# Moving one weight load behind two casts, and the first second products behind two sets of transposes

## The chip, the cores and the metric

The kernel runs on one core of one Trainium2 chip. The metric is device microseconds of one launch, taken as the median of several runs; lower is better. A separate execution is recorded by the hardware profiler, and all engine times below come from that one.

## What is computed

A linear attention with a decay per head is followed by a two-layer network without gating. Four sequences of 768 positions, 8 heads of 64, give 3072 tokens of width 512.

```python
for b in range(nb):                      # blocks of 64 positions
    intra = (qb @ kb.T * Dmask) @ vb     # Dmask[i, j] = lam ** (i - j) for i >= j
    inter = (qb * lam_pow) @ kv_state
    out[block] = intra + inter
    kv_state = lam_block * kv_state + (kb * rev_pow).T @ vb
x = out as (3072, 512)
h = x @ w_in                             # 512 x 2048
g = max(h, 0) + alpha * min(h, 0)
y = g @ w_out                            # 2048 x 512
```

Inputs and the output are float32. Inside, matrix products take float16 and accumulate in float32.

## The kernel before

The tokens are cut into 6 chunks of 512 (two sequences, 256 positions each). A chunk holds four *units*: unit `4c + 2*bi + hh` is sequence `bi` of the chunk's two and head half `hh` (4 heads). So units 4 and 5 share one set of loaded q, k and v (`load(1, 0, ...)`), and units 6 and 7 another (`load(1, 1, ...)`).

Each unit goes through these steps:

- `load(c, bi, x)` (L87) brings q, k or v of two units from HBM, on SyncE's DMA queue: 0.5 MB in float32.
- `cast(n, name, engine)` makes float16 of one unit's k, q or v; the engine is `G` (GpSimd, L252), `A` (ScalarE, L248) or `V` (VectorE, L250).
- `key_decayed(n)` (L278) makes the decayed key.
- `transposes(n, engine)` turns q and k round. For `A` and `V` it is eight TensorE transposes into the PSUM bank `tk` (L306) and a copy out by that engine. For `D` it is a transposing DMA on SyncE's queue (L296). `decayed(n)` (L340) makes the decayed query from the result.
- `cluster(old, new)` is TensorE's attention work: the state's part of `old` (L367), the scores of `new` (L384), scores times v of `old` (L396), and the state's update from decayed key and v of `new` (L411). VectorE masks the scores (L422) and VectorE and ScalarE move the state (L443 to L447); then the output of `old` is copied into `xT`.

Once four units of a chunk are through, the network follows: `up(c, f)` (L479) is one of 16 first products of a chunk, 4 matmuls of 128x512, with ScalarE's part (L487) and VectorE's `slope_product` (L503) behind it. `down(c, t, part, 4)` (L518) is a fourth of the second product for token tile `t`: 4 matmuls that read w_out's quarter `part`. The last part is copied out by ScalarE (L531) and stored by SyncE (L540); with `hold` the store is issued later, by `store_held`. The last chunk uses `down_last` (L547).

Weights are loaded in quarters on GpSimd's DMA queue, with a cast from float32 to float16 under way: `load_win(i)` (L96) and `load_wout(i)` (L102), 0.5 MB each as written. `gate(i, "out")` (L113) is a tiny copy on SyncE's queue that reads a quarter: SyncE stands there until the quarter has landed, and the loads behind it start no earlier.

The order on every engine is the program's order, written out by hand for chunks 0 to 2: each engine, and each DMA queue, takes its instructions as they come in the text and waits on semaphores. Buffers are rotating: 5 sets of raw tiles, 4 of each float16 tile, 3 output tiles; PSUM has banks `op`, `tk`, `acc`, two `h`, and two for scores. GpSimd issues w_out's loads between its casts, so a cast that waits for its data also holds back the loads behind it.

Of the kernel before, what the change touches and what calls it, by code (L numbers as in the profile page):

```python
# [11 lines left out]
def kernel(  # L12
# [67 lines left out]
    def load(c, bi, x, half=None):  # L80

        pb, b = c // 2, 2 * (c % 2) + bi
        if (c, bi) not in raws:
            raws[c, bi] = [raw_pool.tile([128, H, 2 * D], fp32, tag=f"{n}raw", name=f"{n}raw") for n in "kqv"]
        heads = ds(0, H) if half is None else ds(4 * half, 4)
        i = "kqv".index(x)
        nc.sync.dma_start(  # L87
            out=raws[c, bi][i][:, heads, :],
            in_=(k, q, v)[i][b, heads, ds(pb * W, W), :].rearrange("h (p e) d -> p h (e d)", e=2),
        )  # L90
# [10 lines left out]
    def load_wout(i):  # L101
        nc.gpsimd.dma_start(  # L102
            out=w_out_sb[:, ts(i, 4), :],
            in_=moe_w_out[ts(i, 512), :].rearrange("(f p) d -> p f d", p=128),
        )
# [20 lines left out]
    def bank_of(bank, name, dtype=fp32):  # L126
        pool = h_ps_pool if bank == "h" else ps
        return pool.tile([128, CH], dtype, tag=bank, name=name)
# [101 lines left out]
    def query_decay(hp, block):  # L230
        x = qdecay[:, hp // 2, :, hp % 2, ds(block * 64, 64)]
        f = pos_f.rearrange("p (e a j) -> p e a j", e=2, a=2)[:, :, block]
        nc.scalar.activation(x, f, AF.Exp, scale=llp[:, hp : hp + 1])
# [12 lines left out]
    def copy_on(eng, out, in_):  # L246
        if eng == "A":
            nc.scalar.activation(out, in_, AF.Copy)  # L248
        elif eng == "V":
            nc.vector.tensor_copy(out=out, in_=in_)  # L250
        else:
            nc.gpsimd.tensor_copy(out=out, in_=in_)  # L252

    def raw_of(n):
        c, bi, hh = units[n]
        return {
            x + "16": t[:, ds(4 * hh, 4), :].rearrange("p h (e d) -> p e h d", e=2)
            for x, t in zip("kqv", raws[c, bi])
        }

    def cast(n, name, eng):
        t = T.setdefault(n, {})
        if name == "v16":
            t[name] = half_pool.tile([128, 2, 4, D], fp16, tag=name, name=name)
            copy_on(eng, t[name], raw_of(n)[name])
            return
        if "qk16" not in t:
            t["qk16"] = half_pool.tile([128, 2, 2, 4, D], fp16, tag="qk16", name="qk16")
        copy_on(eng, t["qk16"][:, int(name == "k16")], raw_of(n)[name])

    def engine(x):
        return nc.gpsimd if x == "G" else nc.vector

    def key_decayed(n, eng="G"):
        hh = units[n][2]
        kr = raw_of(n)["k16"]
        kdec = half_pool.tile([128, 2, 4, D], fp16, tag="kdec", name="kdec")
        engine(eng).tensor_tensor(  # L278
            out=kdec,
            in0=kr,  # L280
            in1=kdecay[:, ds(4 * hh, 4), :].rearrange("p h e -> p e h").unsqueeze(3).to_broadcast([128, 2, 4, D]),
            op=ALU.mult,
        )
        T.setdefault(n, {})["kdec"] = kdec
# [6 lines left out]
    def transposes(n, eng, decay=True):  # L291

        t = T[n]
        qkT = qkt_pool.tile([128, 2, 2, 2, L], fp16, tag="qkT", name="qkT")
        if eng == "D":
            nc.sync.dma_start(  # L296
                out=qkT.rearrange("p x e h j -> p (x e h) j"),
                in_=t["qk16"].rearrange("p x e h d -> p (x e h d)"),
                transpose=True,
            )  # L300
        else:
            tp = ps.tile([128, 2, 2, 2, L], fp16, tag="tk", name="tp")
            for x in (1, 0):
                for e in range(2):
                    for hp in range(2):
                        nc.tensor.transpose(  # L306
                            tp[:, x, e, hp, :],
                            t["qk16"][:, x, e, ds(2 * hp, 2)].rearrange("p l d -> p (l d)"),
                            ident,
                        )  # L310
            copy_on(eng, qkT, tp)
            t["qps"] = tp[:, 0]
        t["qkT"] = qkT
        if decay:
            decayed(n)
# [19 lines left out]
    def decayed(n, eng="G"):  # L335
        c, bi, hh = units[n]
        t = T[n]
        qdT = qkt_pool.tile([128, 2, 2, L], fp16, tag="qdT", name="qdT")
        p = ds(64, 64) if c < 2 else ds(0, L)
        engine(eng).tensor_tensor(  # L340
            out=qdT[:, :, :, p],
            in0=(t["qps"] if eng == "P" else t["qkT"][:, 0])[:, :, :, p],
            in1=qdecay[:, hh, :, :, p],
            op=ALU.mult,
        )
        t["qdT"] = qdT
# [123 lines left out]
    G = {}  # L470
# [21 lines left out]
    def slope_product(c, f, bi=None):  # L492
        h_ps, m = OPEN.pop((c, f, bi))
        n = CH if bi is None else W
        if (c, f) not in G:
            G[c, f] = g_pool.tile([128, 2, 2, L], fp16, tag=f"g{f}", name=f"g{f}")
        g = G[c, f]
        if bi is None:
            g, mv, hv = g.rearrange("p e b j -> p (e b j)"), m, h_ps
        else:  # L500
            g = g[:, :, bi, :]
            mv, hv = (y[:, 0:n].rearrange("p (e j) -> p e j", e=2) for y in (m, h_ps))
        nc.vector.scalar_tensor_tensor(  # L503
            out=g, in0=mv, scalar=oma[:, f : f + 1], in1=hv, op0=ALU.mult, op1=ALU.add
        )

    def lhs(c, f, t):
        return G[c, f][:, t // 2, t % 2, :]
# [3 lines left out]
    def down(c, t, part, nparts, bank="op", hold=False):  # L512
        if part == 0:
            O[c, t] = bank_of(bank, "o_ps")
        o_ps = O[c, t]
        n = NF // nparts
        for f in range(part * n, part * n + n):
            nc.tensor.matmul(  # L518
                o_ps,
                lhsT=lhs(c, f, t),  # L520
                rhs=w_out_sb[:, f, :],
                start=(f == 0),
                stop=(f == NF - 1),
            )
        if part == nparts - 1:
            store(c, t, o_ps, 0, DM, hold)
            del O[c, t]

    def store(c, t, o_ps, c0, n, hold=False):
        o_sb = o_pool.tile([128, DM], fp32, tag="osb", name="o_sb")  # L530
        nc.scalar.activation(o_sb[:, 0:n], o_ps[:, 0:n], AF.Copy)  # L531
        pb, b = c // 2, 2 * (c % 2) + t % 2
        rows = out[ds(b * S + pb * W, W), ds(c0, n)].rearrange("(j e) d -> e j d", e=2)[t // 2]
        HELD[c, t] = (rows, o_sb[:, 0:n])
        if not hold:
            store_held(c, t)

    def store_held(c, t):
        rows, tile = HELD.pop((c, t))
        nc.sync.dma_start(out=rows, in_=tile)  # L540
# [141 lines left out]
    slope_product(0, 7, None)  # L682
    up(0, 4, None, "h", True)
    slope_product(0, 4, None)
    load_wout(0)
    up(0, 11, None, "op")
    key_decayed(4, "G")
    up(0, 8, None, "tk")
# [3 lines left out]
    up(0, 14, None, "h")  # L692
    cast(4, "v16", "G")
    load(1, 1, "q", None)
    cast(7, "k16", "G")
    cast(5, "k16", "V")
    up(0, 5, None, "op", True)
# [12 lines left out]
    up(0, 12, None, "h", True)  # L710
    cast(6, "k16", "A")
    load_wout(3)
    down(0, 0, 0, 4, "h")
    cast(5, "v16", "G")
    slope_product(0, 12, None)
    gate(3, "in")
    cluster(4, 5, "V", state_first=True)
    cast(6, "q16", "G")
    transposes(6, "A", False)
    key_decayed(6, "G")  # L720
    down(0, 2, 0, 4, "op")
    load(2, 0, "k", None)
    down(0, 3, 0, 4, "h")
    cast(7, "q16", "G")
    transposes(7, "V", False)
    decayed(7, "V")
    decayed(5, "V")
    down(0, 2, 1, 4, "op")
# [4 lines left out]
    cluster(5, 6, "A", state_first=True)  # L733
    decayed(6, "V")
    cast(7, "v16", "A")
    load(2, 1, "q", None)
    cast(11, "q16", "G")
    down(0, 1, 0, 4, "tk")
    down(0, 2, 2, 4, "op")
    down(0, 0, 1, 4, "h")  # L740
    load(2, 0, "q", None)
    cast(9, "k16", "G")
    cast(8, "q16", "G")
    cluster(6, 7, "A")
    load(2, 1, "k", None)
    key_decayed(10, "G")
# [10 lines left out]
    key_decayed(9, "G")  # L757
    up(1, 6, None, "op")
    transposes(8, "D", False)
    load(3, 0, "k", None)  # L760
    down(0, 0, 3, 4, "h", True)
    down(0, 3, 2, 4, "h")
    store_held(0, 0)
    query_decay(1, 0)
    cast(10, "k16", "A")
    decayed(8, "G")
    cast(9, "q16", "A")
    up(1, 5, None, "tk", True)
    transposes(9, "D", False)
    cast(11, "k16", "G")  # L770
    slope_product(1, 5, None)
    up(1, 7, None, "op", True)
# [11 lines left out]
    up(1, 4, None, "op")  # L784
    up(1, 11, None, "h")
    load(2, 1, "v", None)
    cluster(8, 9, "A")
    transposes(10, "D", False)
    up(1, 9, None, "tk")
# [158 lines left out]
```

## Time and profile before

| | us |
|---|---|
| runs: median (lowest to highest of 3) | 215.7 (215.24 to 218.39) |
| the profiled execution, its own time | 217.38 |
| its span, first to last instruction | 215.6 |
| TensorE busy | 206.4 |
| VectorE, ScalarE, GpSimd busy | 131.6, 116.7, 86.8 |
| granted TensorE clock, mean | 0.998 |

The span is what the engine timelines cover; the execution's own time is 1.8 us longer here. In the profile PE is TensorE (PEld its weight loads), DVE VectorE, ACT ScalarE, POOL GpSimd, and SP SyncE; a `q` behind a name means the engine's sequencer. A timeline line gives the start, the length, engine, source line, operation, what it writes and reads, how many were merged, and in brackets how long the engine stood idle before it and what ended that. A wait line gives who waited for whom, microseconds in total, times, and the longest. The DMA digits are the mean busy share of the DMA engines, in tenths, in 40 slices of 5.4 us.

### The profile page before, as it was taken

What the parts mean: (1) busy time and instruction counts of PE and PEld (TensorE: products, weight loads), DVE (VectorE), ACT (ScalarE), POOL (GpSimd) and SP (SyncE); (2) the same over time, 40 slices, a digit from 0 to 9 for tenths busy, and PEclk for the clock granted to TensorE, in tenths of its full rate; (3) what the DMA queues carried; (4) which work ended last, traced back from release to release, by engine and by line L of the source; (5) the groups of instructions that cost most, each with busy time, mean ns of one, the idle gap of its engine ahead of it and who ended that gap; (6) DMA issues with size and microseconds to landing.
All of it is one profiled execution on the core that took longest, in us unless ns stands there. A gap on an engine that the chain in (4) does not pass through costs nothing.

```text
span 215.6 us, 5212 instructions
## 1 busy us (share of the span) xinstructions
PE 206.4 (96%) x2089; PEld 107.3 (50%) x2089; DVE 131.6 (61%) x254; ACT 116.7 (54%) x220; POOL 86.8 (40%) x160
## 2 busy tenths in 40 slices
PE   7998997889999999999999999999999999999993
PEld 7564443445444545455554554554545444444453
DVE  7894887664298969879876645745646344444000
ACT  6996787335776544657855545544434534444121
POOL 7285254503592745577677366357311000000000
PEclk9999999999999999999999999999999999999999
DMA  5999999999999999699549997043011011110212
GB/s 164 295 270 206 244 237 249 160 248 281 240 284 144 294 237 271 161 255 173 71 128 227 249 238 203 13 100 97 2 52 49 14 38 49 50 49 3 97 49 97
DMA packets 62478, 33.90 MB, mean 157 GB/s; under 512 B 18150, under 2 KB 59510, under 8 KB 62454
## 3 DMA queue, kind: packets, MB, share of 16 engines
q1 hardware_dynamic: 58182, 29.37, 56.6%
q0 software_dynamic: 4224, 4.19, 12.1%
q8 instruction: 16, 0.26, 0.5%
q14 instruction: 8, 0.07, 0.1%
q10 hardware_dynamic: 48, 0.01, 0.0%
HBM read 27.27 MB, written 6.29 MB: 156 GB/s over the span
## 4 chain that ended last, share of the span: by engine, by line
PE 72%; DMA 20%; SPq 3%; POOL 2%; ACT 1%; issue 1%; DVE 0%; ACTq 0%
PE o_ps L518 30%; PE h_ps L479 29%; PE o_ps L547 6%; DMA vraw<-in_v_dram 5%; DMA kraw<-in_k_dram 5%; DMA w_in_sb<-in_moe_w_in_dram 5%; DMA w_out_sb<-in_moe_w_out_dram 5%; PE s L384 2%; PE acc L396 2%; SPq L87 2%; PE acc L367 2%; PE acc L411 1%; POOL qk L252 1%; ACT o_sb L531 0%; POOL w_in_sb L96 0%
## 5 line engine op out<-in xcount | busy, mean ns | idle before, releaser
L503 DVE SCALAR_TENSOR_TENSOR g<-m,oma,h_ps 128x512 f16<-128x512 f32 x96 | 70.5, 745 | 55.7 <-ACT m L487 54.2
L479 PE MATMUL h_ps<-xT,w_in_sb 128*128 128x512 f16 x384 | 93.4, 379 | 0.6 <-DMA w_in_sb<-in_moe_w_in_dram 0.4
L487 ACT ACTIVATE m<-h_ps 128x512 f32<-128x512 f32 x96 | 56.9, 597 | 50.6 <-PE h_ps L479 49.0
L518 PE MATMUL o_ps<-w_out_sb,g 128*128 128x512 f16 x320 | 79.5, 379 | 2.3 <-DMA w_out_sb<-in_moe_w_out_dram 2.3
L479 PEld LDWEIGHTS <-w_in_sb 128*128 128x128 f16 x384 | 36.5, 98 | 43.5 <-DMA w_in_sb<-in_moe_w_in_dram 0.6
L518 PEld LDWEIGHTS <-g 128*128 128x128 f16 x320 | 30.3, 98 | 38.1 <-DMA w_out_sb<-in_moe_w_out_dram 1.8
L461 POOL COPY RD<-R 64x128 f16<-64x128 f16 x64 | 19.6, 306 | 41.0 <-DVE R L447 39.3
L422 DVE TENSOR_TENSOR sm<-s,dmask 128x512 f16<-128x512 f32 x48 | 30.8, 683 | 7.3 <-PE s L384 7.0
L340 POOL TENSOR_TENSOR qdT<-qkT,qdecay 128x512 f16<-128x512 f16 (+1 forms) x19 | 20.1, 1059 | 11.8 <-ACT qkT L248 6.0
L531 ACT ACTIVATE o_sb<-o_ps 128x512 f32<-128x512 f32 (+2 forms) x26 | 14.7, 564 | 17.8 <-PE o_ps L547 10.9
L248 ACT ACTIVATE xT<-acc 128x512 f16<-128x512 f32 x21 | 12.5, 597 | 12.1 <-PE acc L411 8.1
L278 POOL TENSOR_TENSOR kdec<-kraw,kdecay 128x512 f16<-128x512 f32 x16 | 17.2, 1075 | 3.0 <-DMA kraw<-in_k_dram 3.0
L547 PE MATMUL o_ps<-w_out_sb,g 128*128 128x512 f16 (+2 forms) x96 | 14.1, 308 | 0.0
L447 DVE SCALAR_TENSOR_TENSOR R<-R,rdecay,acc 128x64 f16<-128x64 f16 x56 | 12.3, 272 | 1.2 <-ACT R L444 1.2
L252 POOL CAST qk<-kraw 128x512 f16<-128x512 f32 x12 | 7.4, 613 | 14.1 <-ACT RD L443 9.7
L547 PEld LDWEIGHTS <-g 128*128 128x128 f16 x96 | 8.1, 98 | 6.1
L252 POOL CAST v<-vraw 128x512 f16<-128x512 f32 x13 | 8.2, 628 | 5.3 <-DMA vraw<-in_v_dram 5.2
L396 PE MATMUL acc<-sm,v 64*64 64x128 f16 x384 | 10.0, 217 | 0.2 <-issue 0.2
L384 PE MATMUL s<-qkT 64*64 64x128 f16 x384 | 10.0, 222 | 0.0
L367 PEld LDWEIGHTS <-RD 128*128 128x128 f16 x80 | 6.4, 98 | 5.8 <-ACT RD L443 0.7
L252 POOL CAST qk<-qraw 128x512 f16<-128x512 f32 x13 | 8.0, 616 | 2.2 <-DMA qraw<-in_q_dram 2.0
L367 PE MATMUL acc<-qdT,RD 128*128 128x128 f16 x80 | 8.4, 219 | 0.0
(67 smaller groups left out, 124.2 us busy)
## 6 DMA issues: line engine op xcount, KB each, us to landing
out_dram<-o_sb SPq DMA_DIRECT2D x23, 256.0 KB, 2.5
qraw<-in_q_dram SPq DMA_DIRECT2D x10, 512.0 KB, 5.6
kraw<-in_k_dram SPq DMA_DIRECT2D x10, 512.0 KB, 7.9
vraw<-in_v_dram SPq DMA_DIRECT2D x10, 512.0 KB, 6.0
w_in_sb<-in_moe_w_in_dram POOLq DMA_DIRECT2D x4, 512.0 KB, 9.4
w_out_sb<-in_moe_w_out_dram POOLq DMA_DIRECT2D x4, 512.0 KB, 9.9
kraw<-in_k_dram SPq DMA_DIRECT2D x4, 256.0 KB, 4.3
qraw<-in_q_dram SPq DMA_DIRECT2D x4, 256.0 KB, 4.5
```

The lines of the kernel that those rows point to most:

```text
L252: nc.gpsimd.tensor_copy(out=out, in_=in_)
L278: engine(eng).tensor_tensor(out=kdec, in0=kr, in1=kdecay[:, ds(4 * hh, 4), :].rearrange("p h e -> p e h").unsqueeze(3).to_broadcast([128, ...
L340: engine(eng).tensor_tensor(out=qdT[:, :, :, p], in0=(t["qps"] if eng == "P" else t["qkT"][:, 0])[:, :, :, p], in1=qdecay[:, hh, :, :, p], ...
L367: nc.tensor.matmul(ot[a][:, hp, :].rearrange("p (e j) -> p e j", e=2), lhsT=RD[bb, ho][:, a, hp].rearrange("p h d -> p (h d)"), rhs=to["qd ...
L422: nc.vector.tensor_tensor(out=sm, in0=s[hl], in1=mask_of(hl, hh), op=ALU.mult)
L461: nc.gpsimd.tensor_copy(out=RD[b, hh][p, a, :, hl, :], in_=R[b, hh, 2 * pb + a][p])
L479: nc.tensor.matmul(h_ps[:, 0:n] if bi is None else h_ps[:, 0:n].rearrange("p (e j) -> p e j", e=2), lhsT=w_in_sb[:, gi, ts(f, 128)], rhs=x ...
L487: nc.scalar.activation(m[:, 0:n], h_ps[:, 0:n], AF.Relu, scale=-1.0)
L503: nc.vector.scalar_tensor_tensor(out=g, in0=mv, scalar=oma[:, f : f + 1], in1=hv, op0=ALU.mult, op1=ALU.add)
L518: nc.tensor.matmul(o_ps, lhsT=lhs(c, f, t), rhs=w_out_sb[:, f, :], start=(f == 0), stop=(f == NF - 1),)
L531: nc.scalar.activation(o_sb[:, 0:n], o_ps[:, 0:n], AF.Copy)
L547: nc.tensor.matmul(o_ps[:, 0:n], lhsT=lhs(c, f, t), rhs=w_out_sb[:, f, ds(x, n)], start=(f == 0), stop=(f == NF - 1),)
```

## The change

Nothing is computed differently; statements change places, and each engine's order with them.

- GpSimd: `load_wout(0)` leaves its place behind unit 5's cast of q, and goes behind unit 5's cast of v. That cast moves ahead of unit 7's cast of k (which waits for its data); before, it stood behind all four w_out loads.
- TensorE: `down(0, 0, 0)` moves from ahead of `cluster(4, 5)` to behind unit 6's transposes, and unit 7's transposes move ahead of `down(0, 2, 0)` and `down(0, 3, 0)`.
- GpSimd and SyncE: units 8 and 9's q (`load(2, 0, "q")`) comes ahead of units 10 and 11's, and unit 8's cast of q ahead of unit 11's. 
- SyncE: k of units 12 and 13 (`load(3, 0, "k")`) moves from between the transposing DMAs of units 8 and 9 to behind `load(2, 1, "v")`; the held store of tile 0 moves behind unit 9's transposing DMA.

```diff
--- before.py
+++ after.py
@@ -682,7 +682,6 @@
     slope_product(0, 7, None)
     up(0, 4, None, "h", True)
     slope_product(0, 4, None)
-    load_wout(0)
     up(0, 11, None, "op")
     key_decayed(4, "G")
     up(0, 8, None, "tk")
@@ -692,6 +691,8 @@
     up(0, 14, None, "h")
     cast(4, "v16", "G")
     load(1, 1, "q", None)
+    cast(5, "v16", "G")
+    load_wout(0)
     cast(7, "k16", "G")
     cast(5, "k16", "V")
     up(0, 5, None, "op", True)
@@ -710,19 +711,18 @@
     up(0, 12, None, "h", True)
     cast(6, "k16", "A")
     load_wout(3)
-    down(0, 0, 0, 4, "h")
-    cast(5, "v16", "G")
     slope_product(0, 12, None)
     gate(3, "in")
     cluster(4, 5, "V", state_first=True)
     cast(6, "q16", "G")
     transposes(6, "A", False)
     key_decayed(6, "G")
+    load(2, 0, "k", None)
+    cast(7, "q16", "G")
+    down(0, 0, 0, 4, "h")
+    transposes(7, "V", False)
     down(0, 2, 0, 4, "op")
-    load(2, 0, "k", None)
     down(0, 3, 0, 4, "h")
-    cast(7, "q16", "G")
-    transposes(7, "V", False)
     decayed(7, "V")
     decayed(5, "V")
     down(0, 2, 1, 4, "op")
@@ -733,14 +733,14 @@
     cluster(5, 6, "A", state_first=True)
     decayed(6, "V")
     cast(7, "v16", "A")
+    load(2, 0, "q", None)
     load(2, 1, "q", None)
+    cast(8, "q16", "G")
     cast(11, "q16", "G")
     down(0, 1, 0, 4, "tk")
     down(0, 2, 2, 4, "op")
     down(0, 0, 1, 4, "h")
-    load(2, 0, "q", None)
     cast(9, "k16", "G")
-    cast(8, "q16", "G")
     cluster(6, 7, "A")
     load(2, 1, "k", None)
     key_decayed(10, "G")
@@ -757,16 +757,15 @@
     key_decayed(9, "G")
     up(1, 6, None, "op")
     transposes(8, "D", False)
-    load(3, 0, "k", None)
     down(0, 0, 3, 4, "h", True)
     down(0, 3, 2, 4, "h")
-    store_held(0, 0)
     query_decay(1, 0)
     cast(10, "k16", "A")
     decayed(8, "G")
     cast(9, "q16", "A")
     up(1, 5, None, "tk", True)
     transposes(9, "D", False)
+    store_held(0, 0)
     cast(11, "k16", "G")
     slope_product(1, 5, None)
     up(1, 7, None, "op", True)
@@ -784,6 +783,7 @@
     up(1, 4, None, "op")
     up(1, 11, None, "h")
     load(2, 1, "v", None)
+    load(3, 0, "k", None)
     cluster(8, 9, "A")
     transposes(10, "D", False)
     up(1, 9, None, "tk")
```

## The prediction

> **What bounds the kernel now.** I read the busy table first, then TensorE's waits, then the timelines of TensorE and GpSimd around the change, then the chain that ended last.
>
> ```profile
> PE 206.4 (96%) x2089; PEld 107.3 (50%) x2089; DVE 131.6 (61%) x254; ACT 116.7 (54%) x220; POOL 86.8 (40%) x160
> DMA  5999999999999999699549997043011011110212
> ```
>
> TensorE is busy for 206.4 of 215.6 us, and the other engines far less. The DMA digits say that up to slice 16 (86 us) transfers run nearly without a break: there, the order of transfers is what can be late. From the list of TensorE's waits (the start-up's left out):
>
> ```profile
> PE o_ps L518 <- DMA w_out_sb<-in_moe_w_out_dram: 2.3, 3, 1.3
> ...
> PE acc L411 <- POOL v L252: 0.6, 1, 0.6
> ```
>
> These two, 2.9 us together, are what the change can touch. Their places on TensorE:
>
> ```profile
> 36.47 1.04 PE L518 MATMUL o_ps<-w_out_sb,g 128*128 128x512 f16 x4 [1.33 <-DMA w_out_sb<-in_moe_w_out_dram]
> ...
> 38.83 0.32 PE L411 MATMUL acc<-v,kdec 64*64 64x64 f16 x16 [0.64 <-POOL v L252]
> 39.08 0.70 PE L306 MATMUL tp<-ident,qk 128*128 128x128 f16 x8
> 39.62 1.89 PE L518 MATMUL o_ps<-w_out_sb,g 128*128 128x512 f16 x8
> ...
> 42.28 1.89 PE L518 MATMUL o_ps<-w_out_sb,g 128*128 128x512 f16 x8 [0.33 <-DMA w_out_sb<-in_moe_w_out_dram]
> ...
> 46.59 1.89 PE L518 MATMUL o_ps<-w_out_sb,g 128*128 128x512 f16 x8 [0.65 <-DMA w_out_sb<-in_moe_w_out_dram]
> ```
>
> Quarters 0, 1 and 2 of w_out are each waited for, and unit 5's v once. After 46.59 TensorE has no gap over 0.15 us but 0.22 at 69.7. The same stretch on GpSimd, which issues w_out:
>
> ```profile
> 26.55 0.79 POOL L102 DMA_DIRECT2D w_out_sb<-in_moe_w_out_dram  x1
> 29.17 2.05 POOL L278 TENSOR_TENSOR kdec<-kraw,kdecay 128x512 f16<-128x512 f32 x2 [1.83 <-DMA kraw<-in_k_dram]
> 31.17 0.80 POOL L252 CAST v<-vraw 128x512 f16<-128x512 f32 x1
> 35.31 0.62 POOL L252 CAST qk<-kraw 128x512 f16<-128x512 f32 x1 [3.34 <-DMA kraw<-in_k_dram]
> 35.87 2.29 POOL L102 DMA_DIRECT2D w_out_sb<-in_moe_w_out_dram  x3
> 38.13 0.64 POOL L252 CAST v<-vraw 128x512 f16<-128x512 f32 x1
> ```
>
> GpSimd stands at the cast of unit 7's k until 35.31; quarters 1 to 3 and unit 5's v wait behind it. From issue to landing the quarters took 9.9, 6.4, 9.9 and 11.3 us (queries of the tile): landed at 36.4, 42.2, 46.6 and 48.7. The chain that ended last agrees: unit 7's k load (23.98, 11.28 us long), its cast, quarter 2's load (36.67, 9.89), then the product at 46.59.
>
> **The change, part by part.** No instruction is added or removed; everything is order, so the sum is of waits. My yardstick is the start of the second product that needs quarter 2, at 46.59 now, because from there TensorE is full.
>
> *GpSimd's queue.* Quarter 0's issue leaves 26.55. Ahead of it now stand two decayed keys (held by a load until 29.17), unit 4's v and unit 5's v. So: 29.17 + 2.05 + 0.80 + 0.60 is 32.5 for its issue, 6 us later than now. Then comes its issue (0.8), unit 7's k (0.6), quarters 1 to 3 from 33.9 to 36.2. That needs unit 7's k raw by 33.3; it lands at 35.26 now, beside quarter 0's half megabyte, which at the 207 to 252 GB/s of the stretches from 30 to 34 us is 2.1 to 2.5 us of transfer. Without it k lands at about 33, and hides. If it doesn't come sooner, quarters 1 to 3 are issued as now. Unit 6's and 7's q casts, now done at 39.3 and 40.9, follow at about 36.8 and 38.5. Unit 5's v is ready at 32.5, so the 0.64 wait goes.
>
> *When quarter 0 lands.* No row has a w_out load at that place. Nearest is quarter 1: issued when the raw loads were almost through, 6.4 us. That gives 38.9. The other bound is quarter 0's own 9.9 beside raw loads: 42.4. In the new order the raw loads have some 1.5 us left at 32.5, so I take 6.6, just above the low end: 39.1.
>
> [...]
>
> *TensorE.* Its first products end at 35.14 (36.47 less 1.33). It next takes the cluster of units 4 and 5, which can start when VectorE frees the accumulator (state rows of 34.92, 0.46 long): 35.45, a new gap of 0.3. The cluster is 1.0 and unit 6's transposes 0.55 (their q at 36.8): 37.1. Then second product (0, part 0) waits for quarter 0: 2.0 us at 39.1. So the wait is not removed, it is moved behind 1.6 us of other work. From there to the yardstick the rows give 0.87 for that product, 0.54 for unit 7's transposes, 1.72 and 1.73 for four products, 0.90 for the cluster of 5 and 6 and 0.97 for the product behind it, 6.73 in all: 45.9.
>
> *Quarters 1 and 2.* Loads of w_in that were queued behind each other landed 2.5 to 2.8 us apart (19.6, 22.1, 24.7, 27.5); quarter 2 came 4.3 after quarter 1. So quarter 1 lands at 41.7 to 43.4 and puts the yardstick at it plus 3.6 (1.73, 0.90 and 0.97): 45.3 to 47.0; quarter 2, at 44.3 to 47.7, is itself the bound. I take 2.6, since now all four are issued back to back as the w_in loads nearly were: 45.3 and 44.3, behind quarter 0's 45.9. The yardstick moves from 46.59 to 45.9: **0.7 us gained**. The bounds are 2.8 gained (no wait left: 35.45 + 1.0 + 0.55 + 6.73 = 43.8, with 0.05 at each wait) and 2.6 lost (quarter 0 at 42.4).
>
> *SyncE's queue.* The k load of units 12 and 13 leaves 56.07 and stands behind the v load of 61.91, ahead of the transposes of units 10 and 11. At 290 GB/s (the stretch 72 to 74) it is 1.8 us of transfer. Unit 10's transposed tile now lands at 70.28, and TensorE reads it at 71.95: 1.67 of cover.
>
> ```profile
> 61.91 0.46 SPq L87 DMA_DIRECT2D vraw<-in_v_dram  x1
> 62.48 5.15 SPq L296 DMA_TRANSPOSE qkT<-qk  x2
> ...
> 70.44 1.17 POOL L340 TENSOR_TENSOR qdT<-qkT,qdecay 128x512 f16<-128x512 f16 x1 [2.41 <-DMA qkT<-qk]
> ```
>
> Both sides come 0.7 earlier, since SyncE there waits for an output row of TensorE's. So the cover is short by 0.13; with latency I take **0.2 lost**. Bounds: nothing, if the load fits into gaps, and 0.9, if SyncE's issue of 0.6 is added. The load is due in VectorE's row at 73.14 and lands near 70: hidden. The q, v and k loads behind come 1 us later. ScalarE waits for them at 72.98, 76.57 and 79.75, and is idle for 1.97 before its output copy at 83.38: covered.
>
> *The rest.* The swapped q loads and casts of units 8 to 11 give unit 8's transpose its data about 1 us sooner; TensorE has no gap there to lose. The held store goes behind unit 9's transpose, which waits for a ScalarE cast ending at 57.97; the copy that needs the store's buffer comes after 83. Free, unless that transpose comes over 10 us late.
>
> Sum: -0.7 + 0.2 = -0.5. The profiled execution took 217.38 with a span of 215.6, so 216.9 and 215.1 with the change; its own time is 1.7 above the runs' median of 215.7, so I forecast 215.2 for the median.
>
> **Rivals.**
> [...]
> - *w_out later (slower).* Quarter 0 goes out 6 us later, and TensorE has only 1.6 us to put ahead of it. Beyond a landing at 39.8 (6.73 before 46.59) each us late is a us lost. At its old 9.9 us it costs 2.6: 218.3; if instead quarter 1 follows 4.3 behind, 0.5: 216.2. For it: three of four rows took 9.9 or more. Against: those ran beside raw loads or two other quarters.
> - *Unit 10 late (slower).* The cover of 1.67 is used up at unit 10: up to 0.9 instead of 0.2, and with no gain at w_out 216.6.
> - *The change does nothing.* The 3.34 wait of GpSimd stays because k lands no sooner. Then quarters 1 and 2 are as now and the yardstick stays: 215.9.
>
> **How the numbers follow.** Forecast 0.45, all cover 0.12, w_out later 0.23, unit 10 late 0.1, nothing 0.1. The range runs from 213.3, into all cover, to 217.4, into w_out later; the forecast's own is 214.6 to 216.0. About 2% (4.3 us) is what a measurement of this kernel can tell from no change, the three runs lying 3.1 apart. More than 4.3 gained is more than all TensorE's waits: 0.01. More than 4.3 lost needs quarter 0 after 44.1, longer than any row, or a stall that I don't see: 0.04. Within: 0.95.
>
> **What would show it.** Right: quarter 0 issued near 32.5 and landed near 39; no wait on v at L411; one w_out wait near 2 us ahead of the first second product, small ones after; unit 7's k cast without a wait; at most 0.3 ahead of unit 10's scores. Wrong: a w_out wait over 2.7, three waits as now, or a new gap over 0.5 us after 50.

## The result

| | runs | median us | lowest to highest |
|---|---|---|---|
| before | 4 | 215.47 | 214.58 to 218.39 |
| changed | 4 | 218.43 | 217.08 to 219.68 |

The ratio is 1.0145 (95% interval 1.0097 to 1.0194): the change made the kernel slower, by 3 us between these medians of four, where 0.5 us of gain was forecast. (A repeat further down gives 1.4 us.) The granted clock of each execution matters here: the four changed ones were granted 0.992, 0.992, 1.000 and 0.984 of TensorE's clock, and took 218.0, 218.8, 217.1 and 219.7. In the comparisons further down the slowest executions are left out of the ratio, so I give beside it how many executions lost clock.

The profiled execution of the changed kernel took 218.03 with a span of 216.3. Its busy times, and TensorE's waits in the stretch of the change (a third, 0.2 for unit 6's q, is in the timeline):

```profile
PE 208.1 (96%) x2089; PEld 107.7 (50%) x2089; DVE 131.1 (61%) x254; ACT 116.7 (54%) x220; POOL 86.4 (40%) x160
```

```profile
PE o_ps L518 <- DMA w_out_sb<-in_moe_w_out_dram: 1.8, 1, 1.8
PE acc L367 <- DVE R L447: 0.4, 1, 0.4
```

The waits fell, as forecast: three on w_out and one on v (2.9 us) became one on w_out of 1.8 and 0.4 for the accumulator. But TensorE's busy time rose by 1.7 us for the same 2089 matmuls, and slice 7 (38 to 43 us) of the granted clock, which read 9 before, reads 7. The line of before, then that of the changed kernel:

```profile
PEclk9999999999999999999999999999999999999999
```

```profile
PEclk9999999799999999999999999999999999999999
```

TensorE's timeline there:

```profile
35.75 0.27 PE L367 MATMUL acc<-qdT,RD 128*128 128x128 f16 x2 [0.39 <-DVE R L447]
...
37.26 0.40 PE L306 MATMUL tp<-ident,qk 128*128 128x128 f16 x4 [0.21 <-POOL qk L252]
39.41 1.02 PE L518 MATMUL o_ps<-w_out_sb,g 128*128 128x512 f16 x4 [1.76 <-DMA w_out_sb<-in_moe_w_out_dram]
40.27 0.90 PE L306 MATMUL tp<-ident,qk 128*128 128x128 f16 x8
40.97 5.05 PE L518 MATMUL o_ps<-w_out_sb,g 128*128 128x512 f16 x16
...
46.75 2.76 PE L518 MATMUL o_ps<-w_out_sb,g 128*128 128x512 f16 x12
```

The cluster, the transposes and the wait stand where the prediction put them. Then 16 matmuls take 5.05 us; as two groups of eight they took 1.89 each before. For that stretch alone, the tile's line gives minimum, median and maximum of one matmul, and the table by stretches gives TensorE's clock in the third column from the end:

```profile
L518 PE MATMUL o_ps<-w_out_sb,g x16: 379/380/634, 41.0 to 45.6; 128*128 128x512 f16 x16
```

```profile
38.00:40.00 2.00, 0.59 (x3) 0.29 (x3) 1.10 (x4) 0.78 (x1) 0.75 (x2) 1.00 1.22 198
40.00:42.00 2.00, 2.00 (x14) 1.24 (x12) 0.69 (x1) 0.00 (x0) 0.00 (x0) 0.61 1.14 168
42.00:44.00 2.00, 2.00 (x7) 0.70 (x5) 1.70 (x4) 0.00 (x0) 0.00 (x0) 0.54 1.21 204
44.00:46.00 2.00, 2.00 (x12) 0.89 (x10) 0.00 (x0) 0.00 (x0) 0.00 (x0) 1.00 1.25 205
```

A granted 0.61 and 0.54 over two times 2 us are 1.7 us of clock lost, or 3.4 us at half clock: read in short stretches, it is 0.50 from 40.44 to 43.85 and 1.00 on both sides. That costs the 1.7 us by which TensorE's busy time rose. GpSimd's timeline shows the queue as forecast, with no wait at unit 7's k:

```profile
29.68 2.06 POOL L278 TENSOR_TENSOR kdec<-kraw,kdecay 128x512 f16<-128x512 f32 x2 [3.28 <-DMA kraw<-in_k_dram]
31.68 1.36 POOL L252 CAST v<-vraw 128x512 f16<-128x512 f32 x2
32.99 0.79 POOL L102 DMA_DIRECT2D w_out_sb<-in_moe_w_out_dram  x1
33.78 0.62 POOL L252 CAST qk<-kraw 128x512 f16<-128x512 f32 x1
34.34 2.25 POOL L102 DMA_DIRECT2D w_out_sb<-in_moe_w_out_dram  x3
```

The yardstick of the prediction, the start of the second product that needs quarter 2, is 0.97 behind 46.75 (the first four of the twelve matmuls there read quarter 0): 47.72, against 46.59 before and 45.9 forecast. From there to the end is 168.6 us, against 169.0 before.

### The profile page after: what moved, and what is told of

Its sections match the earlier page's. It is cut to its first block, busy times and chain, and to the rows that moved or that the text cites. A ratio compares the mean times of both kernels' runs of the same rounds, so it can differ in the third digit from the quotient of the medians.

```text
span 216.3 us, 5210 instructions
## 1 busy us (share of the span) xinstructions
PE 208.1 (96%) x2089; PEld 107.7 (50%) x2089; DVE 131.1 (61%) x254; ACT 116.7 (54%) x220; POOL 86.4 (40%) x160
## 4 chain that ended last, share of the span: by engine, by line
PE 80%; DMA 13%; POOL 2%; SPq 2%; issue 0%; ACT 0%; ACTq 0%
PE o_ps L518 33%; PE h_ps L479 32%; PE o_ps L547 6%; DMA w_in_sb<-in_moe_w_in_dram 5%; DMA w_out_sb<-in_moe_w_out_dram 3%; PE s L384 3%; DMA kraw<-in_k_dram 3%; DMA vraw<-in_v_dram 3%; PE acc L396 2%; PE acc L367 2%; SPq L87 1%; PE acc L411 1%; POOL kdec L278 1%; POOL v L252 1%; POOL w_in_sb L96 0%; PE tp L306 0%
## 5 line engine op out<-in xcount | busy, mean ns | idle before, releaser
L518 PE MATMUL o_ps<-w_out_sb,g 128*128 128x512 f16 x320 | 80.6, 385 | 1.8 <-DMA w_out_sb<-in_moe_w_out_dram 1.8
L518 PEld LDWEIGHTS <-g 128*128 128x128 f16 x320 | 30.8, 99 | 38.1 <-issue 3.8
L278 POOL TENSOR_TENSOR kdec<-kraw,kdecay 128x512 f16<-128x512 f32 x16 | 16.7, 1048 | 3.7 <-DMA kraw<-in_k_dram 3.7
L547 PEld LDWEIGHTS <-g 128*128 128x128 f16 x96 | 8.1, 98 | 6.1
```

The costliest lines, as they stand in the source:

```text
L278: engine(eng).tensor_tensor(out=kdec, in0=kr, in1=kdecay[:, ds(4 * hh, 4), :].rearrange("p h e -> p e h").unsqueeze(3).to_broadcast([128, ...
L518: nc.tensor.matmul(o_ps, lhsT=lhs(c, f, t), rhs=w_out_sb[:, f, :], start=(f == 0), stop=(f == NF - 1),)
L547: nc.tensor.matmul(o_ps[:, 0:n], lhsT=lhs(c, f, t), rhs=w_out_sb[:, f, ds(x, n)], start=(f == 0), stop=(f == NF - 1),)
```

## Experiments

Two theories to begin with. *Clock*: the wait, now in one piece behind small matmuls, makes TensorE lose half its clock for 3.4 us. *Landing*: quarter 0 comes later, and that alone is the loss. A third, that the moved loads do it, was to be ruled out.

**The kernel before again.** No edit.

> The kernel before, unchanged, to get the span and granted clock of each of its executions. If the clock theory holds (the changed kernel loses because TensorE's clock is halved for 3.41 us behind its long wait for w_out), the kernel before is granted 0.998 or more in nearly every execution and lies near 215.5. If the kernel before loses clock as often (two or three executions of four under 0.995), the clock is not what separates the two. The profiled execution of before (217.38, span 215.6) lies 1.9 above its median; if it is typical of the profile alone, all executions with a span show 215 to 216; if it was an unlucky one, most spans lie near 213.7.

Twelve executions, median 215.88; lost clock (under 0.995; the others I call at full clock) in 3 of them, and in 10 of the 87 executions of the same kernel that ran beside all the experiments. So it loses clock too, but in about one execution of eight. Against itself its ratio read 1.0034 (1.0002 to 1.0066): a difference of 0.3% between kernels means nothing here. The profiled execution took 215.01, with a span of 213.2, 2.4 us below the profile that the prediction used. GpSimd's timelines tell the two apart; here it is in the new one:

```profile
32.16 0.61 POOL L252 CAST qk<-kraw 128x512 f16<-128x512 f32 x1 [0.88 <-DMA kraw<-in_k_dram]
32.72 2.29 POOL L102 DMA_DIRECT2D w_out_sb<-in_moe_w_out_dram  x3
```

Unit 7's k landed at 32.1 and not at 35.3, so quarters 1 to 3 went out 3 us sooner; quarter 1 was waited for until 41.09, and quarter 2 not at all. The DMA engines show it too. The last two numbers of each line are their busy share (as this table counts it, it can pass 1) and GB/s, first for the old profile of before, then for the new one:

```profile
36.00:38.00 2.00, 1.53 (x38) 0.96 (x39) 0.69 (x2) 0.29 (x1) 2.00 (x3) 1.00 0.66 155
```

```profile
36.00:38.00 2.00, 2.00 (x62) 1.46 (x61) 1.16 (x3) 0.37 (x3) 0.85 (x2) 1.00 1.23 238
```

In the old profile the engines moved 155 GB/s between the raw loads and the late w_out loads; in the new one 238. One kernel, two courses, and the prediction was made on the worse.

**Filler in the wait.**

```diff
     cast(7, "q16", "G")
+    fill(8, "op")
     down(0, 0, 0, 4, "h")
```

> The changed kernel with eight matmuls of no use (1.73 us at full clock) where TensorE waited 1.76 us for quarter 0. Clock theory: no half clock near 40 us, granted clock 0.998 or more in nearly every execution, the product behind unit 7's transposes at 379 ns each again, and a time 1.3 to 1.7 below the changed kernel, 216.7 to 217.1. Rival, the late landing alone: nothing changes, 218 to 218.8, since the filler takes the time of the wait.

Median 216.81; none of 12 executions lost clock (lowest 0.997). Even the profiled one, in which TensorE still stood 1.18 us for quarter 0 behind the filler, kept its clock:

```profile
38.56 1.89 PE L141 MATMUL unread<-ident 128*128 128x512 f16 x8
41.63 1.02 PE L518 MATMUL o_ps<-w_out_sb,g 128*128 128x512 f16 x4 [1.18 <-DMA w_out_sb<-in_moe_w_out_dram]
42.49 0.61 PE L306 MATMUL tp<-ident,qk 128*128 128x128 f16 x8
42.94 3.62 PE L518 MATMUL o_ps<-w_out_sb,g 128*128 128x512 f16 x16
```

On the same chip the first part of the change, next below, took 218.47; the rest of the change, below that, has no effect that shows. So useless work in the wait gained 1.7 us, and no execution lost clock: the clock theory holds. But 216.81 is still above before (ratio 1.0069, 1.0039 to 1.0100), so something else is left.

**The first part alone.** w_out's quarter 0, unit 5's v and TensorE's order as changed; the later loads, casts and stores as before.

> Only the first part of the change: w_out's quarter 0 behind unit 5's cast of v, and the first second products behind the transposes; the later loads, casts and stores as before. If the loss is made at w_out (clock or landing): as the changed kernel, 218 to 218.8, with clocks of 0.984 to 0.992 in most executions. If it is made by the moved k load or the swapped q loads: near the kernel before, 215 to 216.

Median 218.47, with 8 of 12 executions at 0.992 or 0.984. The profiled one waited 3.19 us for quarter 0 and lost twice the clock:

```profile
38.00:40.00 2.00, 0.00 (x0) 0.00 (x0) 1.00 (x4) 0.44 (x1) 0.36 (x1) 0.79 1.00 147
40.00:42.00 2.00, 1.55 (x4) 0.56 (x4) 0.00 (x0) 0.00 (x0) 0.00 (x0) 0.50 1.21 192
42.00:44.00 2.00, 2.00 (x12) 1.31 (x11) 0.69 (x1) 0.00 (x0) 0.00 (x0) 0.50 1.24 206
44.00:46.00 2.00, 2.00 (x7) 0.65 (x5) 1.70 (x4) 0.00 (x0) 0.00 (x0) 0.50 1.24 207
```

The lost shares, 0.21 and three times 0.50 of 2 us, are 3.4 us, so 6.8 us at half clock. The four executions at full clock had a median of 217.1. The loss is all in this part, as far as the noise lets one see.

**The later part alone.**

> Only the later part: k of units 12 and 13 behind the v load, q loads and casts swapped, the held store moved; w_out and the first second products as before. If the loss is made at w_out: as the kernel before, 215 to 216, within 0.3%. If the moved loads make it: 217 or more, with a new wait of TensorE after 50 us.

Median 215.66, ratio 1.0022 (0.9993 to 1.0051), no lost clock: no effect that can be told from none, and from the yardstick to the end it takes 168.6 us, as the others do.

**Quarter 0 back at its old place.**

```diff
     slope_product(0, 4, None)
+    load_wout(0)
...
     cast(5, "v16", "G")
-    load_wout(0)
```

> The changed kernel with one statement put back: quarter 0 of w_out is issued at its old place, ahead of the two decayed keys. Theory now (quarter 0's late landing costs by itself, since it is the bound of the products behind it, and the wait in one piece costs half clock on top): quarter 0 lands near 35.7, the products wait for quarter 1 (near 41) at most, no execution under 0.995 at the rate of before, 215 to 216. Rival (TensorE's new order loses by itself, wherever the load is): stays at 217 or more.

Median 216.73, and 5 of 12 executions lost clock; the 7 others have 215.59. Half a miss. Putting the load back brings the time at full clock to within noise of before, but TensorE's new order still gathers idle time. In the profiled execution no product waited for quarter 0, and unit 7's k landed late, at 35.5; GpSimd's later cast of q was then waited for at unit 6's transposes, 2.07 us, in front of every second product. Before, a product stood ahead of them.

**GpSimd's part alone.** `cast(5, "v16", "G")` and `load_wout(0)` as changed; TensorE's order and the rest as before.

> The kernel before with GpSimd's part of the change alone: unit 5's cast of v moved ahead and quarter 0 behind it; TensorE's order and the later loads as before. Theory: TensorE stands from 35.1 to near 39.5 in one piece, 4.3 us; the cluster and transposes (1.6 us) come behind it, so it is about 1.5 us worse than the changed kernel at full clock and loses clock in most executions: 219 to 221. Rival (the order on TensorE is the loss): better than the changed kernel, 215 to 217.

Median 219.93, 5 of 6 lost clock; the profiled execution waited 3.3 us in one piece. By the medians TensorE's new order earned 1.5 us of what quarter 0's later issue cost. The one execution at full clock took 217.0, no more than the first part's 217.1, so much of that may be clock.

**Unit 5's cast alone.** The kernel before with `cast(5, "v16", "G")` ahead of `cast(7, "k16", "G")`.

> The kernel before with nothing but unit 5's cast of v moved ahead of unit 7's waiting cast of k. The wait for v at line 411 (0.64 us in the profile of before, 2.0 in another execution) goes. Where GpSimd's wait for unit 7's k is short (k landing at 32.1), nothing is gained; where k lands at 35.2, w_out's quarter 2 still decides. Theory: 214.7 to 215.4, no more than 0.3 below before. Rival (the v wait is on the path of most executions): 0.6 to 2 below.

Median 216.02, above the 214.7 to 215.4 expected, ratio 1.0029 (1.0000 to 1.0058), no clock lost in 12: no gain, and by the noise above no loss either.

**Quarters 1 to 3 ahead of unit 7's k.** As the last one, and also:

```diff
     cast(5, "v16", "G")
+    load_wout(1)
+    load_wout(2)
+    load_wout(3)
     cast(7, "k16", "G")
```

> The kernel before with unit 5's cast of v and then quarters 1 to 3 of w_out ahead of unit 7's waiting cast of k; quarter 0 and TensorE's order as before. Theory: the loads no longer hang on when unit 7's k lands (32.1 in one execution, 35.3 in two others), so the executions with a late k go: issue of quarter 1 near 32.5 always, median 214.2 to 214.8 and fewer executions over 215.5. Rival (the three loads take the DMA engines from the raw loads, and q and k of units 6 and 7 come late): new waits at the transposes of units 6 and 7, 215.5 or more.

Median 215.22, ratio 1.0010 (0.9982 to 1.0038), no clock lost in 12. Quarter 1 went out at 32.0 without waiting for k, and the profiled execution reached the yardstick as fast as the good course of before. But the median did not move. Were the late k of the first profile the usual course, this should have gained some 1.7 us; so the medians speak for the good course as the usual one. The profiles do not. Of the five profiled executions with quarter 0 at its old place and the other quarters behind unit 7's k, four have k late, its cast starting at 35.2 to 35.6, and only the second profile of before has it at 32.2. This is the later part alone:

```profile
35.23 0.61 POOL L252 CAST qk<-kraw 128x512 f16<-128x512 f32 x1 [3.37 <-DMA kraw<-in_k_dram]
```

Each of the four lies above its kernel's median (for quarter 0 back at its old place, the median at full clock) by 0.6 to 1.7 us, and the second profile of before lies 0.9 below. So the late course is slow, but how often it comes is open.

**The changed kernel again, and a filler of small matmuls.** The second has 32 matmuls of 128 columns in the place of the eight of 512: `fill(8, "op", None, 128)`.

> The changed kernel, unchanged, beside the two below on one chip, for the count of executions that lose clock. Clock theory: more than half of its executions under 0.995, and a median near 218.4; the ones at 0.995 or more lie 1.2 to 1.8 below the others, near 217. Rival (the three of four were chance): under a quarter lose clock.

> The changed kernel with filler of the same length in the wait, but made of 32 matmuls of 128 columns in place of eight of 512. If any work of TensorE keeps its clock: no execution under 0.995, near 216.8, as with the 512-wide filler. If work in small matmuls counts for less in what grants the clock (the 4 us ahead of the halving hold clusters and transposes, all small): some executions under 0.995 remain, 217 to 218.4.

The changed kernel has a median of 216.80 against 215.38 for before, 1.4 more, and 5 of 12 lost clock, 8 of 16 with the first four; not more than the half that was expected, but four times as often as before. The seven at full clock lie from 215.15 to 217.07 (median 216.18), the five others from 218.39 to 220.44. The profiled one kept its clock behind a wait of 1.82, where the first profile lost it behind 1.76:

```profile
39.18 1.02 PE L518 MATMUL o_ps<-w_out_sb,g 128*128 128x512 f16 x4 [1.82 <-DMA w_out_sb<-in_moe_w_out_dram]
40.04 0.61 PE L306 MATMUL tp<-ident,qk 128*128 128x128 f16 x8
40.48 3.62 PE L518 MATMUL o_ps<-w_out_sb,g 128*128 128x512 f16 x16
...
44.84 2.76 PE L518 MATMUL o_ps<-w_out_sb,g 128*128 128x512 f16 x12
```

So a wait of this length costs clock in one execution and not in another. The small filler had no lost clock in 12, where the changed kernel had 5: small matmuls hold the clock too. What lost it was the idle time, not the small matmuls beside it. Its profile has no wait left:

```profile
36.96 1.95 PE L136 MATMUL unread<-ident 128*128 128x128 f16 x32
38.75 1.03 PE L518 MATMUL o_ps<-w_out_sb,g 128*128 128x512 f16 x4
```

But the filler's median is 217.34, above the changed kernel's 216.80 on this chip, which by itself lies inside the forecast's range; the means are 217.2 and 217.5. The filler takes away the executions over 218.4 and gains 0.3 on average here, where it gained 1.5 (means of 216.9 against 218.4 for the first part) on the other chip. Both fillers stay 1.8 to 2.0 us above before by the medians without any lost clock, but part of that may be the filler's own time: here TensorE was busy with it until 38.75, and quarter 0 had landed by then. Means of the kernels without filler divide the loss better. Over all executions the changed kernel is 1.8 us above before; with those at full clock alone, on both sides, 0.6. The first part, on the other chip, is 3.0 and 1.7 above. So lost clock costs about 1.2 us on average, and 0.6 to 1.7 is something else, most likely quarter 0's later landing: with the load back at its old place the executions at full clock were within noise of before. (If the executions that keep their clock are those with the shorter waits, the 0.6 and 1.7 are too low.) How late quarter 0 lands varies: by 38.75 in this filler's profile (215.9), at 39.4 in the changed kernel's (218.0, clock halved), 41.6 in the first filler's (218.6, full clock, with a start-up 1.5 us longer).

**Quarter 1 earlier still.** As the version with quarters 1 to 3 moved, but `load_wout(1)` right behind `key_decayed(5, "G")`, unit 6's transposes behind `down(0, 2, 0)` and unit 7's behind `down(0, 2, 1)`.

> A try at a better version: on top of quarters 1 to 3 ahead of unit 7's cast of k, quarter 1 goes out right behind the decayed key of unit 5, and units 6's and 7's transposes go behind one more product each. Theory (the landing of quarters 0 and 1 is the bound, 0.5 to 0.9 us of waits each in the execution with the three loads early): quarter 1 lands near 39.5 in place of 40.7, its wait of 0.9 goes, 214.2 to 214.9, below the kernel before. Rival (the earlier load takes the DMA engines from units 6 and 7's q): a wait of 1 us or more at their transposes, 215.2 or more.

A clear miss: median 220.25, ratio 1.0210 (1.0155 to 1.0265), 4 of 6 lost clock. Quarter 1 was waited for until 41.14, no sooner than 40.77 in the version with the three loads early. TensorE stood 0.95 us for GpSimd's cast of q at unit 6's transposes, and then for v:

```profile
46.60 0.32 PE L411 MATMUL acc<-v,kdec 64*64 64x64 f16 x16 [2.44 <-DVE v L250]
```

No version here beats the kernel before by more than its noise.

## Why the prediction was wrong, point by point

- *GpSimd's queue: right.* Quarter 0's issue was forecast at 32.5 and came at 32.99; unit 7's k at about 33 and at 33.2; unit 6's and 7's q casts ended 0.4 and 0.3 later than forecast.
- *Quarter 0's landing: right.* 39.1 forecast, 39.4 measured (6.4 us after issue, where 6.6 was taken); 39.1 to 40.4 in the repeated and first-part runs. The shortest w_out load in the first profiles of the two kernels took 6.4, with other transfers under way.
- *Quarters 1 and 2: right.* 42.4 and 45.3, 0.7 and 1.0 behind the forecast's 41.7 and 44.3, and not waited for.
- *The wait of TensorE: right.* 2.0 forecast, 1.8 measured, and 0.4 for the accumulator in place of 0.3.
- *6.73 us from quarter 0 to the yardstick: wrong, the first step that failed.* It took 8.31 (39.41 to 47.72), because the durations were taken at full clock, and the clock was halved. At full clock it held: 39.18 to 45.81 is 6.63 in the repeated run. A gathered wait was priced by its length only.
- *The 46.59 that it was held against: wrong, the second step.* It came from an execution that took 217.38, 1.7 above its kernel's median, and the gain over it was taken off that median as if the median had the same waits. From the end of the first products to the yardstick:

| execution | us | unit 7's k landed |
|---|---|---|
| before, profile of the prediction | 11.45 | 35.3 |
| before, second profile | 9.76 | 32.1 |
| changed, clock halved | 12.36 | 33.2 |
| changed, full clock | 10.36 | not shown |

  Against the first row the change does earn 1.1 at full clock; the forecast was 0.7. Against the second it loses 0.6, and that row is one of the changed kernel's quicker executions; the means at full clock put the loss at 0.6 for the changed kernel and 1.7 for the first part. The 3.34 us wait at unit 7's cast, on which the gain was built, was 0.88 in the second profile; that it is what sets the 217.38 apart from the median is likely and not shown, since three of the other profiles have a wait of 2.5 to 3.4 there too.

  The two steps, 1.6 and 1.7, about make up the 3.2 by which 218.43 lies above the forecast of 215.2. That the clock took so much of this median is partly chance: three of the result's four executions lost clock, and 5 of 12 on the repeat, whose median is 1.6 above the forecast.
- *Unit 10's transpose: right in kind, too high.* Its tile landed at 72.08 and was read at 72.61, so 0.5 of the cover was left and the 0.2 was not lost. The later part alone showed no loss.
- *The rivals.* "w_out later" had the right side, and by luck a price near the outcome, 218.3: it counts from a landing past 39.8, and quarter 0 landed at 39.4. (In the first part's profile it landed at 40.4, so there some of that rival is in it.) "All cover", the end of the range with no wait left, was not seen: in the four profiled executions without filler that issue quarter 0 late, TensorE stood for it until 39.18 to 40.45, with 1.8 to 3.3 us of wait. The clock was in no rival.

The length of a wait alone does not tell here whether clock is lost: a wait of 1.76 us, with 0.6 of shorter gaps in the same 4 us, lost it in the first profiled execution of the changed kernel, one of 1.82 kept it in the second, and 8 of 16 executions of that kernel lost it. The time at half clock was 3.4 us in the first of these profiles and 6.8 in the first part's; what sets it was not tried.

What stays open: why unit 7's k lands at 32 or at 35 with the same program. In the second profile of before the raw loads ran at 289 GB/s from 28 to 30 us, in the first at 239; what slowed them was not tried. How often each course comes is open too, and with it why the first profile lay 1.7 us above the median.

## What to carry to other kernels

A wait that is moved is not moved for free: with four waits of 0.3 to 1.3 us between products the profiled execution of before kept its clock in this stretch, and with one of 1.8 that of the changed kernel lost another 1.7 us to it. By count, 13 of 99 executions of the kernel before lost clock and 8 of 16 of the changed one. Price a gathered wait with its clock, and where it can't go, fill it (worth 1.5 us on average on one chip here, and 0.3 on another). Before a forecast is built on a wait in one profiled execution, compare that execution's own time with the median; where it lies 1 or 2 us above, the wait may be what makes it untypical.

## What I had not expected of the hardware

- TensorE's clock was halved for 3.4 us behind an idle gap of 1.76 us in one execution, and kept behind one of 1.82 in another; eight useless 128x512 matmuls, or 32 of 128 columns, kept it in 24 of 24 executions.
- A 0.5 MB load of w_out landed between 6.4 and 11.9 us after its issue in the first profiles of the two kernels, with other loads queued beside it each time.
- The same program has two courses in its loads: unit 7's k landed at 32.1 us in one profiled execution of before and at 35.3 in the other, and of the 2.4 us between the two 1.7 lie from the end of the first products to the yardstick.
